# A Strassen feed-forward after sparse attention: the scheme used inside three chunks instead of four, with weight sums made one chunk later and fetched earlier

## The chip, the cores and the metric

One core of a Trainium2 chip runs one program that computes everything below. The metric is the device time of one execution in microseconds. Smaller is better.

## The reference, cut to what matters

```python
q, k, v: (8, 8, 576, 64)          # batch, heads, tokens, head width
mask_local   = (rel >= 0) & (rel < 32)                  # heads 0 to 3
mask_strided = (rel >= 0) & (pos_k % 32 == pos_q % 32)  # heads 4 to 7
attn = softmax(where(mask, q @ k.T / 8, -1e9)); y = attn @ v
x  = y.transpose(0, 2, 1, 3).reshape(8, 576, 512)
xn = (x - mean) / sqrt(var + 1e-6) * g_ln
out = x + relu(xn @ w_ch1) @ w_ch2        # 512 -> 2048 -> 512
```

## The kernel before, in words

The 4608 tokens are nine chunks of 512: chunks 0 to 7 are the first 512 tokens of each batch, chunk 8 gathers the last 64 of all eight. The layer norm is folded into the first weights and into a factor on each output row, so that a chunk needs only x, transposed, as TensorE's moving operand. For float32 accuracy each operand is split into a high and a low part, and every product is three matmuls: high by high, high by low, low by high. The 2048 hidden units are 16 blocks f. A plain step (`plain`, one f) runs 12 matmuls of 512 columns into `ph` (the first layer), has ScalarE write `hh` (relu, high part) and VectorE `hl` (low part), and runs 12 matmuls of 512 columns for the second layer of the block before (`run_groups`, tiles `po`). `ph` has one buffer.

Chunk 0 and chunk 1 are plain in the kernel before. Chunks 2 to 5 compute their first layer by Strassen's scheme alone, inside the chunk (`pair`): two blocks f together, tokens in two halves of 256 columns, seven products of six 256-column matmuls each (`product2`, tiles `x`) instead of eight, with sums of weight blocks as some stationary operands. Chunk 6 is plain; chunks 7 and 8 use the scheme on both chunks together.

The sums of weights (`w_sums`) are made by GpSimd in chunk 1, eight times six instructions, from tiles of the pool `tkp` (seven buffers), and stored to DRAM (`sd`); `a_store` stores the low parts of other weight blocks (`ad`) to make room, and `move`, on ScalarE, copies a weight half once that store has landed. Later, `stage_w(n)` fetches a set of sums from `sd` into a `tkp` tile `sw`, and `split_w(n)` splits it: ScalarE writes the high part, GpSimd the low part.

Attention of the batch that the chunk after next needs runs in between: four pieces a chunk, each for a pair of heads (`now` for its products with v, `nxt` for its scores). A piece is, in order: scores and products on TensorE into `m` and `n` (`s_blocks`, `v_blocks`); on VectorE the masks (`s_mask`), the maximum, and the division by the sums (`v_divide`, tile `xo`); GpSimd subtracts, ScalarE takes the exponential; VectorE transposes the result by 32-blocks and SyncE (SP) stores it (`p_turned`, DRAM tensor `pd`); `p_load` reads it back as `pt`, which the next piece's products need; `v_store` stores `xo` to DRAM (`xdl`, `xds`), and `x_raw` reads that back transposed for `x_blocks`. In plain chunks a generator (`pieces`) hands out these steps, four to each f; a short piece takes three f, a long one four.

The order of instructions on each engine is that of the code. The DMAs of SP's queue, and those that ScalarE issues, are issued in that order too, and an issuing engine stands still until what the next DMA waits for has come.

Within one `pair(c, p)` the order is: for even p the piece; products a11 (into tile x1), s2 (x2), s1 (x3), then a12 onto x1, s3 onto x2, a22 (x4, in x1's bank) and s4 onto x3, with one group of second-layer matmuls after each and two at the end. `Quarter` writes a quarter of the hidden block from x1 (`q`), from sums in SBUF (`q22`, `q21`) or from `u2` (`late`): the high part on ScalarE, `low()` on VectorE. VectorE's sums `add2` build `u2`, `u3` and `p1`.

Of the kernel before, what the change touches and what calls it, by code (L numbers as in the profile page):

```python
# [9 lines left out]
F32 = mybir.dt.float32  # L10
# [53 lines left out]
def kernel(  # L64
# [268 lines left out]
    class Pair:  # L333
# [84 lines left out]
        def t_piece(self):  # L418

            if self.local:  # L420
                self.qt, self.kt = qt_l, kt_l
                nc.vector.transpose(qt_l[:, 0:S], self.raw[:, 0])
                nc.vector.transpose(kt_l[:, STR:STR + S], self.raw[:, 1])
            else:
                self.qt, self.kt = qt_s, kt_s
                for i, dst in enumerate((qt_s, kt_s)):
                    nc.vector.transpose(
                        dst[:, 0:S].rearrange("p (r t) -> p t r", t=NB),
                        self.raw[:, i].rearrange("p (t r) -> p t r", r=STR))

# [160 lines left out]
        def x_raw(self, eng):  # L591

            self.xraw = tkp.tile([P, CH], F32, tag="tk", name=f"xraw{self.id}")
            x_b = (xd_l if self.local else xd_s)[self.b]
            for j in range(4):
# [6 lines left out]

        def x_blocks(self, xT=None):

            cc = self.h0 // 2
            if xT is not None:
# [5 lines left out]
            else:  # L612
# [3 lines left out]
                if d == 0 and (self.b > 2 or j):  # L616
                    stage_sums(j)
# [455 lines left out]
    def pieces(i0, i1):  # L1073
        for i in range(i0, i1):
            now = pairs[i] if i >= 2 * NHP else None
            nxt = pairs[i + 1] if i + 1 < NP else None
            short = i < 3 * NHP - 1 or i >= NP - NHP
# [32 lines left out]
            elif now:  # L1110
                now.x_blocks()
            yield
            yield
            yield
            if not short:
# [3 lines left out]
    gen = pieces(2 * NHP - 1, 3 * NHP)  # L1119
# [53 lines left out]
    def s_split(n):  # L1173
# [5 lines left out]
    xa_t = [xtp.tile([P, NCC, CH], F32R, tag=t, name=f"{t}_a") for t in ("xh", "xl")]  # L1179
    low1 = [w1s[f][:, :, 0:HC] for f in range(1, NFC, 2)]  # L1180
    high1 = [w1s[f][:, :, HC:CH] for f in range(1, NFC, 2)]
    slots = dict(zip(("s2", "s1", "s3", "s4"), (*(t[:, 3].rearrange("p (i x) -> p i x", i=2) for t in xa_t),
                                               *low1[6:])))
# [30 lines left out]

    def half_c(c, step):

        if c == 1:
            at, late = (10, 11, 12, 13), 2
        elif c < wide - 1:
            at, late = (4, 5, 8, 9), 2  # L1220
        else:
            at, late = (4, 5, 7, 8), 3
        if step in at:
            res[c].append([x_load(c, at.index(step))])
        if step - late in at:
            i = at.index(step - late)
            res[c][i].append(x_scale(res[c][i][0], f"{c}_{i}"))
# [20 lines left out]
    def plain(c, n_end):  # L1248
        for f in range(NFC):
            if c == 1 and f == NFC - 1:  # L1250
# [330 lines left out]
```

## Time and profile before

| | us |
|---|---|
| median of the runs | 970.07 (969.98 to 970.16, 2 runs) |
| the profiled execution | 968.79 |
| its span, first to last instruction | 967.0 |
| TensorE busy in the span | 889.5 (92%) |
| VectorE, ScalarE, GpSimd busy | 550.8, 285.5, 353.6 |
| mean granted clock of TensorE | 0.975 of full speed |

Busy times are sums over the whole span; what stands still where is seen only by cutting the span into the chunks' stretches.

### The profile page before, as it was taken

The page shows a single profiled execution, that of the slowest core. Times are in us where ns is not written, and L with a number is a line of the kernel's source. Part 1 is how long each engine was busy: PE and PEld are TensorE (multiplying, and loading weights), DVE is VectorE, ACT ScalarE, POOL GpSimd, SP SyncE. Part 2 cuts the span into 40 slices and gives each one's busy share as a digit, 9 for nine tenths or more (in the row PEclk, how much of TensorE's full clock was granted, in tenths as well). Part 3 has the DMA queues.
Part 4 walks back from the last instruction along what each step waited for, and adds up shares of the span by engine and source line. Part 5 has one row for each costly group of instructions (what it writes and reads, how often), then busy time and mean ns, then how long its engine had stood idle before and what let it go on. Part 6 is the DMA issues. An engine that isn't in the chain of part 4 may idle for free. (4 is left out here: it accounts for less than half of the span.)

```text
span 967.0 us, 20717 instructions
## 1 busy us (share of the span) xinstructions
PE 889.5 (92%) x7981; PEld 739.1 (76%) x7981; DVE 550.8 (57%) x1167; ACT 285.5 (30%) x590; POOL 353.6 (37%) x424
## 2 busy tenths in 40 slices
PE   7899998998799988999899988998979999999997
PEld 6688886786587777887677777777868887878786
DVE  6799954544565657556566557456645544242443
ACT  4786621111232233222422233222212221211121
POOL 5787745565434345243524244232202011112000
PEclk9899999999799999999999999999989999999999
DMA  9999664888677567866677666867676425331021
GB/s 185 230 275 275 178 109 113 203 178 201 125 202 160 142 138 180 203 141 146 138 206 153 150 132 194 187 137 185 164 170 121 96 87 160 102 102 63 1 87 44
DMA packets 383850, 146.64 MB, mean 152 GB/s; under 512 B 297860, under 2 KB 362248, under 8 KB 383752
## 3 DMA queue, kind: packets, MB, share of 16 engines
q1 hardware_dynamic: 300424, 130.44, 53.7%
q10 hardware_dynamic: 83328, 14.89, 8.5%
q8 instruction: 63, 1.03, 0.4%
q14 instruction: 35, 0.29, 0.1%
HBM read 104.56 MB, written 40.70 MB: 150 GB/s over the span
## 5 line engine op out<-in xcount | busy, mean ns | idle before, releaser
L903 PE MATMUL po<-w,hq 128*128 128x512 f32 x768 | 215.1, 396 | 10.7 <-ACT hq L1314 5.6
L903 PE MATMUL po<-w,hh 128*128 128x512 f32 x640 | 204.1, 401 | 0.0
L903 PEld LDWEIGHTS po<-w,hq 128*128 128x128 f32 x768 | 130.1, 190 | 28.5 <-ACT hq L1314 7.5
L903 PEld LDWEIGHTS po<-w,hh 128*128 128x128 f32 x640 | 121.3, 193 | 25.3 <-issue 0.3
L1301 PE MATMUL x<-xh_b,w 128*128 128x256 f32 x512 | 114.3, 286 | 18.0 <-DVE hq L1317 16.5
L903 PE MATMUL po<-w,hl 128*128 128x512 f32 x320 | 126.9, 396 | 0.0
L1301 PEld LDWEIGHTS x<-xh_b,w 128*128 128x128 f32 x512 | 88.1, 190 | 30.7 <-DVE hq L1317 22.0
L1245 POOL TENSOR_TENSOR w<-sw,w 128x256 fp32r<-128x256 f32 x64 | 46.4, 746 | 110.0 <-ACT w L1244 105.9
L498 POOL TENSOR_TENSOR sm<-sm,mx 128x640 f32<-128x640 f32 (+1 forms) x31 | 39.3, 1269 | 100.9 <-DVE mx L493 61.8
L871 DVE SCALAR_TENSOR_TENSOR hl<-ph,hh 128x512 fp32r<-128x512 f32 x48 | 32.9, 686 | 71.6 <-ACT hh L866 71.6
L1301 PE MATMUL x<-xl_b,w 128*128 128x256 f32 x256 | 72.2, 282 | 0.0
L903 PEld LDWEIGHTS po<-w,hl 128*128 128x128 f32 x320 | 61.4, 192 | 13.4
L1245 POOL TENSOR_TENSOR xh_a<-sw,xh_a 128x256 fp32r<-128x256 f32 x32 | 23.6, 737 | 129.2 <-ACT xh_a L1244 118.0
L744 POOL TENSOR_TENSOR rs<-rs,mhalf 128x1 f32<-128x1 f32 x36 | 20.2, 560 | 128.2 <-DVE rs L743 128.1
L866 ACT ACTIVATE hh<-ph 128x512 fp32r<-128x512 f32 x48 | 28.5, 594 | 106.4 <-PE ph L861 87.6
L1301 PEld LDWEIGHTS x<-xl_b,w 128*128 128x128 f32 x256 | 48.7, 190 | 4.7
L854 PE MATMUL ph<-xh,w 128*128 128x512 f32 x124 | 49.8, 401 | 0.0
L504 ACT ACTIVATE sm<-sm 128x648 f32<-128x648 f32 (+1 forms) x32 | 23.8, 744 | 87.3 <-POOL sm L498 87.3
L1176 POOL TENSOR_TENSOR rings<-stage,rings 128x512 fp32r<-128x512 f32 x16 | 20.6, 1289 | 77.8 <-ACT rings L1175 77.8
L854 PE MATMUL ph<-xl,w 128*128 128x512 f32 x124 | 48.4, 391 | 0.0
L1317 DVE SCALAR_TENSOR_TENSOR hq<-p,hq 128x256 fp32r<-128x256 f32 x32 | 16.0, 500 | 54.0 <-ACT hq L1314 54.0
L1244 ACT ACTIVATE xh_a<-sw 128x256 fp32r<-128x256 f32 x32 | 13.4, 417 | 96.0 <-DMA sw<-sd 90.9
(228 smaller groups left out, 1858.4 us busy)
## 6 DMA issues: line engine op xcount, KB each, us to landing
s<-in_moe_w_ch_dram SPq DMA_DIRECT2D x32, 512.0 KB
sw<-sd SPq DMA_DIRECT2D x64, 256.0 KB
out_dram<-x SPq DMA_DIRECT2D x32, 256.0 KB
raw<-in_q_dram SPq DMA_DIRECT2D x108, 72.0 KB
raw<-in_k_dram SPq DMA_DIRECT2D x108, 72.0 KB
wd<-w SPq DMA_DIRECT2D x24, 256.0 KB
ringa<-wd SPq DMA_DIRECT2D x24, 256.0 KB
xds<-xo SPq DMA_DIRECT2D x32, 162.0 KB
```

The source lines that it names most:

```text
L498: eng.tensor_tensor(out=sm, in0=sm, in1=mx[:, :, 0:nt].unsqueeze(3).broadcast_to([P, 2, nt, sm.shape[3]]), op=ALU.subtract)
L504: nc.scalar.activation(out=self.smv, in_=self.smv, func=AF.Exp, scale=SCALE)
L744: nc.gpsimd.tensor_tensor(out=rs, in0=rs, in1=mhalf, op=ALU.pow)
L854: nc.tensor.matmul(ph, w1h[:, cc], x[:, cc, :], start=(new and n == 0 and i == 0), stop=False)
L866: nc.scalar.activation(out=hh, in_=ph, func=AF.Relu)
L871: nc.vector.scalar_tensor_tensor(out=hl, in0=ph, scalar=0.0, in1=hh.bitcast(F32), op0=ALU.max, op1=ALU.subtract)
L903: nc.tensor.matmul(po[c, i], hx, w, start=(n_po[c, i] == 0 and n == 0), stop=(n_po[c, i] == NFC - 1 and n == 2))
L1176: nc.gpsimd.tensor_tensor(out=t[:, :, 1], in0=stage[n], in1=t[:, :, 0].bitcast(F32), op=ALU.subtract)
L1244: nc.scalar.activation(out=w[:, 0], in_=t[:, k], func=AF.Copy)
L1245: nc.gpsimd.tensor_tensor(out=w[:, 1], in0=t[:, k], in1=w[:, 0].bitcast(F32), op=ALU.subtract)
L1301: nc.tensor.matmul(ps, wx, xx[:, j], start=(start and j == 0 and i == 0), stop=(j == 1 and i == 2), skip_group_check=not start)
L1317: nc.vector.scalar_tensor_tensor(out=self.h[1], in0=self.src, scalar=0.0, in1=self.h[0].bitcast(F32), op0=ALU.max, op1=ALU.subtract)
```

## The change

Chunk 2 becomes a plain chunk, and Strassen's scheme alone starts with chunk 3 (`FIRST`). The sums of weights are made in chunk 2 instead of chunk 1, at f = 1, 2, 5, 6, 7, 9, 10, 11 instead of 0, 1, 3, 4, 6, 7, 9, 10; the moves of weight halves stay at f = 3, 7 and 11. In the pairs, `stage_w` for a set of sums is issued one pair earlier; `x_raw` is issued in two halves and lands in `xo` for batches 4 to 6; the divisions that read bank `n` come ahead of the masks; the two transposes of q and k stand on both sides of `q.low()`; `v_sums` stands behind `q22.low()`; the row statistics of two token blocks stand together. The whole weights are stored three times a chunk instead of twice. In chunk 6 the first and the last piece are long instead of short.

```diff
-            for j in range(4):
+            for j in js:
...
+        def x_room(self):
+            if 3 < self.b < B - 1:
+                self.xraw = self.xo.rearrange("p t h d -> p (t h d)")[:, 0:CH]
+            else:
+                self.xraw = tkp.tile([P, CH], F32, tag="tk", name=f"xraw{self.id}")
...
-            short = i < 3 * NHP - 1 or i >= NP - NHP
+            short = i < 3 * NHP - 1 or i in (29, 30)
+            later = i in (3 * NHP, 3 * NHP + 1)
...
-    gen = pieces(2 * NHP - 1, 3 * NHP)
+    gen = pieces(2 * NHP - 1, 4 * NHP)
...
+    LOADS.update({2: (12, 13, 13, 14), **{u: (4, 5, 8, 9) for u in range(FIRST, wide - 1)}})
+    SCALES.update({2: (14, 15, 15, NFC), **{u: (7, 7, 11, 11) for u in range(FIRST, wide - 1)}})
...
-            if c == 1:
+            if c == 2:
                 if f in SUMS_AT:
...
-    SUMS_AT = 0, 1, 3, 4, 6, 7, 9, 10
+    SUMS_AT = 1, 2, 5, 6, 7, 9, 10, 11
+    plain(1, NT)
...
-    plain(1, 1)
+    plain(2, 1)
...
+            now.v_divide(av[0:2])
+            if not nxt.local:
+                parts[0:2] = parts[1], parts[0]
             nxt.s_mask(parts)
-            late_low()
-            now.v_divide(av)
+            now.v_divide(av[2:])
             now.v_store()
             nxt.s_max()
-        else:
-            late_low()
+        late_low()
...
+        if n + 3 < n_end:
+            stage_w(n + 3)
         run_groups(1)
...
-        if fetch:
-            stage_w(n + 2)
...
-        if not even:
-            pairs[i + 2].t_piece()
+        turn = pairs[i + 2].t_pieces() if not even else iter(())
+        next(turn, None)
         run_groups(1)
         product2(p, "a12", "b21", x1, False)
         q = Quarter(c, 2 * p, 0, x1)
         q.low()
-        if fetch:
-            split_w(n + 2)
+        next(turn, None)
         if even:
             nxt.p_turned()
+        if n + 2 < n_end:
+            split_w(n + 2)
+        if even:
+            now.x_raw(nc.scalar, range(2))
...
+        q22 = Quarter(c, 2 * p + 1, 2, p1_t)
         if even:
-            now.x_raw(nc.scalar)
-        q22 = Quarter(c, 2 * p + 1, 2, p1_t)
+            now.x_raw(nc.scalar, range(2, 4))
...
-        if fetch:
-            stage_w(n + 3)
...
-        if even:
-            nxt.v_sums()
         add2(u3_t, x4, u3_t)
         q21 = Quarter(c, 2 * p + 1, 0, u3_t)
         q22.low()
+        if n + 4 < n_end:
+            stage_w(n + 4)
+        if even:
+            nxt.v_sums()
...
-    for c in range(2, wide - 1):
+    for c in range(FIRST, wide - 1):
```

Three places show how instructions moved.

The first is SP's queue in chunk 1, f = 0 to 2: `sd` and `ad` are the stores of the sums and of weight halves, `out_dram` the results of chunk 0, `pd` and `pt` the turned softmax of the next pair. Before:

```order
L814 DMA sd<-f_0_2199 128x2x256
L816 DMA sd<-f_0_2201 128x256 x2
L1230 DMA ad<-w_1_856 256x1x256
L880 DMA out_dram<-x_0_1846 128x512
L880 DMA out_dram<-x_1_1825 128x512
L880 DMA out_dram<-x_2_1793 128x512
L880 DMA out_dram<-x_3_1946 128x512
L628 DMA pd_206<-sm_192 32x4x192 x4
L642 DMA pt_2_2256<-pd_206 128x6x32 x4
```

The same queue now, in chunk 1 and then in chunk 2, f = 1 and 2:

```order
L893 DMA out_dram<-x_3_1946 128x512
L641 DMA pd_206<-sm_192 32x4x192 x4
L655 DMA pt_2_2242<-pd_206 128x6x32 x4
...
L641 DMA pd_207<-sm_191 32x4x160 x4
L363 DMA raw_1_3309<-in_q_dram 32x18x32 x4
L363 DMA raw_1_3309<-in_k_dram 32x18x32 x4
L827 DMA sd<-f_0_3318 128x2x256
L829 DMA sd<-f_0_3320 128x256 x2
L1243 DMA ad<-w_1_856 256x1x256
L827 DMA sd<-f_1_3363 128x2x256
L829 DMA sd<-f_1_3365 128x256 x2
L1243 DMA ad<-w_3_1033 256x1x256
```

No store of sums is left in chunk 1; in chunk 2 the first ones stand behind the `pd` stores of their step, and a piece has four steps instead of three until its `pt` is read.

The second place is ScalarE in an even pair (chunk 4, p = 2); `w` and `xh_a`, `xl_a` are the high parts that `split_w` writes, `hq` the quarters, `xraw` or `xo` the target of `x_raw`. Before:

```order
L1348 COPY p_2144<-x_4_2_6299 128x256
L1244 ACTIVATE w_13_1844<-sw_6188 128x256
L1244 ACTIVATE w_15_2016<-sw_6188 128x256
L504 ACTIVATE sm_191<-sm_191 128x2x6x54
L1314 ACTIVATE hq_4_0_6352<-x_4_2_6299 128x256
L1244 ACTIVATE xh_a<-sw_6331 128x256
L1244 ACTIVATE xl_a<-sw_6331 128x256
L600 DMA xraw_0_6375<-xdl 32x16x32 x4
L1314 ACTIVATE hq_5_2_6380<-p_2144 128x256
```

Now:

```order
L1369 COPY p_2142<-x_4_2_5940 128x256
L1257 ACTIVATE w_13_1844<-sw_5763 128x256
L1257 ACTIVATE w_15_2016<-sw_5763 128x256
L507 ACTIVATE sm_191<-sm_191 128x2x6x54
L1334 ACTIVATE hq_4_0_5993<-x_4_2_5940 128x256
L1257 ACTIVATE xh_a<-sw_5843 128x256
L1257 ACTIVATE xl_a<-sw_5843 128x256
L604 DMA xo<-xdl 32x16x32 x2
L1334 ACTIVATE hq_5_2_6018<-p_2142 128x256
L604 DMA xo<-xdl 32x16x32 x2
```

Two of the four DMAs now stand behind `hq_5_2` (`q22`); the tiles `sw` are the same in kind, but their DMAs stand half a pair to a pair earlier on SP.

The third place is VectorE in an odd pair (chunk 4, p = 3): `staged` is `x_blocks`, `qt_l` and `kt_l` the transposes of `t_piece`, `hq_6_0` is `q.low()`, BN the row statistics. Before:

```order
L615 STREAM_TRANSPOSE staged_2685<-xraw_0_6375 128x256 x2
L739 BN_STATS st_0_6459<-x_0_6328 128x6
L741 BN_AGGR mv_0_6461<-st_0_6459 128x2
L743 TENSOR_SCALAR rs_0_6463<-mv_0_6461 128x1
L422 STREAM_TRANSPOSE qt_l<-raw_1_6179 128x576
L423 STREAM_TRANSPOSE kt_l<-raw_1_6179 128x576
L1317 SCALAR_TENSOR_TENSOR hq_6_0_6489<-x_4_3_6424,hq_6_0_6489 128x256
```

Now:

```order
L628 STREAM_TRANSPOSE staged_3656<-xo 128x256 x2
L427 STREAM_TRANSPOSE qt_l<-raw_1_5820 128x576
L1337 SCALAR_TENSOR_TENSOR hq_6_0_6121<-x_4_3_6064,hq_6_0_6121 128x256
L427 STREAM_TRANSPOSE kt_l<-raw_1_5820 128x576
```

One transpose and the statistics have left the place ahead of `hq_6_0`; both blocks' statistics now stand between `q22.low()` and the `add2` that reads x3.

## Rows read from the trace of the kernel before

**Rows 1.** Windows by stage: length, TensorE busy (instructions), granted clock, DMA share, GB/s.

```profile
143.61:251.26 107.65, 98.33 (x885) 0.95 0.71 170
251.26:367.47 116.21, 100.42 (x994) 0.94 0.68 152
367.47:473.81 106.34, 95.87 (x993) 1.00 0.70 164
473.81:582.72 108.91, 97.86 (x993) 0.98 0.69 160
582.72:692.79 110.07, 100.52 (x1013) 1.00 0.73 172
692.79:786.65 93.86, 88.71 (x770) 0.96 0.53 122
```

**Rows 2.** Windows of single plain steps: PE, PEld, DVE, ACT, POOL busy, clock, DMA.

```profile
174.84:180.29 5.45, 5.45 (x26) 4.50 (x24) 1.19 (x2) 1.74 (x3) 5.14 (x7) 1.00 0.57 153
734.53:741.96 7.43, 7.43 (x141) 6.03 (x140) 4.68 (x13) 1.27 (x3) 0.42 (x1) 1.00 0.45 93
708.61:723.65 15.04, 9.89 (x141) 7.81 (x140) 5.39 (x13) 1.86 (x3) 1.28 (x1) 0.77 0.73 171
```

**Rows 3.** Windows of an even and an odd Strassen pair of chunk 3.

```profile
395.77:407.01 11.24, 10.89 (x70) 9.54 (x67) 6.83 (x19) 2.13 (x5) 2.66 (x3) 1.00 0.96 238
407.01:421.74 14.73, 13.23 (x183) 10.97 (x182) 8.69 (x22) 5.17 (x14) 8.42 (x12) 1.00 0.74 151
```

**Rows 4.** Timeline of TensorE: first matmuls of two products of 256 columns.

```profile
402.10 0.28 PE L1301 MATMUL x<-xh_b,w 128*128 128x256 f32 x1
...
403.50 0.28 PE L1301 MATMUL x<-xh_b,w 128*128 128x256 f32 x1
```

**Rows 5.** Waits of TensorE in 143.61:251.26 (chunk 1): us, times, longest.

```profile
PE n L521 <- DMA pt<-pd: 9.3, 5, 3.8
```

**Rows 6.** Timeline in chunk 1: VectorE's turned softmax, SP's stores behind it.

```profile
154.33 0.97 DVE L624 STREAM_TRANSPOSE sm<-sm 128x768 f32<-128x768 f32 x1
...
156.72 0.39 SPq L814 DMA_DIRECT2D sd<-f  x1
...
161.15 2.43 SPq L628 DMA_DIRECT2D pd<-sm  x4
```

**Rows 7.** Window of GpSimd in chunk 1: one set of sums.

```profile
174.20:180.00 5.80, 5.49 (x8) 1.00 0.51 139
```

**Rows 8.** Timeline of ScalarE: the first move of a weight half.

```profile
177.33 0.63 ACT L1200 ACTIVATE w<-w 128x512 fp32r<-128x512 f32 x1 [12.82 <-DMA ad<-w]
```

**Rows 9.** Waits of TensorE in 251.26:367.47 (chunk 2): the first pieces' `pt`.

```profile
PE n L521 <- DMA pt<-pd: 2.6, 1, 2.6
PE n L521 <- DMA raw<-in_q_dram: 1.1, 1, 1.1
```

**Rows 10.** Waits of TensorE in 367.47:473.81 (chunk 3).

```profile
PE x L1301 <- DVE hq L1317: 3.8, 3, 1.8
PE m L452 <- DVE u L1306: 1.7, 2, 0.9
PE x L1301 <- DVE xo L571: 1.7, 3, 1.0
PE po L903 <- DVE x L877: 1.5, 1, 1.5
PE po L903 <- ACT hq L1314: 1.2, 2, 0.7
PE x L1301 <- DVE p L1306: 0.9, 1, 0.9
```

**Rows 11.** Timeline in chunk 3, p = 2 and 3: a fetch of sums, ScalarE behind it.

```profile
402.52 0.41 SPq L1238 DMA_DIRECT2D sw<-sd  x1
...
407.23 0.42 ACT L1244 ACTIVATE xh_a<-sw 128x256 fp32r<-128x256 f32 x1 [5.25 <-DMA sw<-sd]
...
409.56 0.42 ACT L1314 ACTIVATE hq<-p 128x256 fp32r<-128x256 f32 x1 [1.60 <-issue]
```

**Rows 12.** Timeline of VectorE in chunk 3, p = 3: a transpose ahead of `q.low()`.

```profile
414.21 0.77 DVE L422 STREAM_TRANSPOSE qt_l<-raw 128x576 f32<-128x576 f32 x1
```

More of the change, by code (lines that the diff above doesn't have):

```diff
@@ L418, in t_piece, with t_pieces @@
         def t_piece(self):
[L420 to L423, printed above, removed]
-            else:
-                self.qt, self.kt = qt_s, kt_s
-                for i, dst in enumerate((qt_s, kt_s)):
+            for _ in self.t_pieces():
+                pass
+        def t_pieces(self):
+            self.qt, self.kt = (qt_l, kt_l) if self.local else (qt_s, kt_s)
+            for i, dst in enumerate((self.qt, self.kt)):
+                if self.local:
+                    nc.vector.transpose(dst[:, STR * i:STR * i + S], self.raw[:, i])
+                else:
                     nc.vector.transpose(
@@ L589, in v_store, with x_raw @@
                     nc.sync.dma_start(x_b[c, :, :, cs], xov[64 * c:64 * c + GS, 0:nt])
-        def x_raw(self, eng):
-            self.xraw = tkp.tile([P, CH], F32, tag="tk", name=f"xraw{self.id}")
+        def x_raw(self, eng, js=range(4)):
+            if 0 in js:
+                self.x_room()
             x_b = (xd_l if self.local else xd_s)[self.b]
-            for j in range(4):
+            for j in js:
                 c0 = P * self.n0 + 32 * j
@@ L1109, in pieces @@
                 now.x_blocks(whole[f"b{1 + cc // 2}1{cc % 2}"])
-            elif now:
+            elif now and not later:
                 now.x_blocks()
@@ L1114, in pieces @@
             yield
+            if later:
+                now.x_blocks()
             if not short:
@@ L1213, in back @@
         nc.sync.dma_start(w1s[f].bitcast(F32)[:, :, HC:CH], wd[p][:, 2])
+    LOADS, SCALES = ({u: at for u in range(1, wide)} for at in ((4, 5, 7, 8), (7, 8, 10, 11)))
+    LOADS.update({2: (12, 13, 13, 14), **{u: (4, 5, 8, 9) for u in range(FIRST, wide - 1)}})
+    SCALES.update({2: (14, 15, 15, NFC), **{u: (7, 7, 11, 11) for u in range(FIRST, wide - 1)}})
     def half_c(c, step):
-        if c == 1:
[L1218 to L1227, printed above, removed]
+        for d, steps in ((c, step), (c - 1, step + NFC)):
+            for i in range(NT):
+                if LOADS.get(d, ())[i:i + 1] == (steps,):
+                    res[d].append([x_load(d, i)])
+                if SCALES.get(d, ())[i:i + 1] == (steps,):
+                    res[d][i].append(x_scale(res[d][i][0], f"{d}_{i}"))
     def a_store(p):
@@ L1249, in plain @@
         for f in range(NFC):
-            if c == 1 and f == NFC - 1:
+            if c == 2 and f == NFC - 1:
                 for name in OPERANDS[0:3]:
@@ L1255, in plain @@
             h = hh, h_low(c, f, ph, hh)
-            if c == 1 and f in MOVED:
+            if c == 2 and f in MOVED:
                 move(f)
@@ L1330, in pair @@
         last, more = p == NFC // 2 - 1, c < wide - 2
-        n = NFC * (c - 2) + 2 * p
-        fetch = n < NFC * (wide - 3) - 2
+        n = NFC * (c - FIRST) + 2 * p
+        n_end = NFC * (wide - 1 - FIRST)
         i = NHP * (c + 1) + p // 2
@@ L1387, in pair @@
         add2(p1_t, x3, u3_t)
+        q22 = Quarter(c, 2 * p + 1, 2, p1_t)
         if even:
-            now.x_raw(nc.scalar)
-        q22 = Quarter(c, 2 * p + 1, 2, p1_t)
-        if not even and i + 3 < NP:
+            now.x_raw(nc.scalar, range(2, 4))
+        elif i + 3 < NP:
             pairs[i + 3].load_qk()
-        if fetch:
-            stage_w(n + 3)
         if last:
```

28 lines of the change are left out of this document (18 added, 10 removed).

## The prediction

> **What bounds the kernel now.** I cut the span into the chunks' stretches first [rows 1], since the busy share of the whole says only that TensorE is busy most of the time. In every stretch TensorE is the engine with the most work, and in every stretch of chunks 1 to 5 it stands still or runs slowly for a good part. To see how much, I took undisturbed pieces of its work. A plain step without attention takes 5.45 us for 24 matmuls of 512 columns, 0.227 us each; with a piece of attention it takes 7.43, so a piece costs 1.98 [rows 2]. Two successive Strassen products begin 1.40 us apart [rows 4]; less three matmuls of 512 columns that leaves 0.72 for six of 256 columns, 0.120 each.
>
> From these I work out floors. A Strassen pair has 42 matmuls of 256 columns and 24 of 512: 5.04 + 5.45 = 10.49; eight pairs and four pieces make 83.9 + 7.9 = 91.8 for a chunk. A plain chunk is 16 x 5.45 + 7.9 = 95.1. Against 91.8 the Strassen chunks take 116.2, 106.3, 108.9 and 110.1 [rows 1]; the last holds 7 groups more (7 x 0.68 = 4.8). The excess is 24.4, 14.5, 17.1 and 13.5. So each chunk in which the scheme stands alone is slower than a plain chunk without waits would be. Chunk 1, plain, has a floor of 94.0 for its stretch (15 steps, four and a half pieces, and 3.4 of the last step) and takes 107.65: an excess of 13.6.
>
> Then I asked what ended the waits. In chunk 1 all is `pt`: 9.3 us in 5 waits [rows 5], and the granted clock of 0.95 [rows 1] says that some of the stretch ran at 1.2 GHz instead of 2.4 after them. The timeline shows why: VectorE began to turn the softmax at 154.33, but SP issued its `pd` store only at 161.15, since the stores of the sums stood ahead of it from 156.72 on [rows 6]. In chunk 3 the waits are many and small: six kinds sum to 10.8 of the 14.5 [rows 10]; what is left is the restart after each.
>
> **The change part by part.**
>
> *Chunk 2 plain.* It removes 8 x 42 matmuls of 256 columns (336 x 0.120 = 40.3) and adds 192 of 512 (43.6): 3.3 us more on the path. By rows alone the scheme was worth that and no more here. The Trainium skill, "TensorE: Matmul & The Clock Gate", section "Wait — 56ns, not 53.3ns?", says that matmuls follow each other at the columns over 2.4 GHz plus about 2.5 ns. That would be an estimated 0.109 and 0.216 us, and giving up the scheme would cost an estimated 4.7 us; the rows show 0.120 and 0.227, so the sum goes by 3.3.
>
> *Chunk 1 without sums.* Eight sets of sums, 5.5 us of GpSimd each [rows 7], and 32 DMAs on SP leave it. `pd` then stands behind the four result stores alone, which are issued while the transposes still run; 6.8 us of lateness [rows 6] are more than the longest wait of 3.8 [rows 5]. I take 1 us of excess instead of 13.6; bounds 0 to 4 (one wait of the longest kind).
>
> *Chunk 2 with the sums.* The same work meets a plain chunk again, but a piece now has four steps until its `pt` is read, one step or 5.45 us more than the pieces of chunk 1 had, and the longest wait there was 3.8 [rows 5]; the first `sd` stores stand behind `pd`. What is late next is ScalarE: the first move of a weight half stood until 177.33, 12.8 us, for the `ad` store [rows 8], and the first sums now start one step later (f = 1) while the move stays at f = 3. Behind the move are queued the next `hh`, and on VectorE the transposes of the delayed `x_blocks`, which write into the freed half, and `hl`; `ph` has one buffer, so the next first layer waits for both. I expect short waits there, at f = 4 and f = 8. Bounds: nothing, and the 13.6 of chunk 1 before. I take 5, nearer the lower end, because GpSimd needs 8 x 5.5 = 44 us of a stretch of 93.
>
> *The first Strassen chunk.* Chunk 2 before has 24.4 of excess, 9.9 more than chunk 3; it starts with `pt` and `raw` waits of 2.6 and 1.1 us [rows 9] and a granted clock of 0.94 over the stretch [rows 1]. Now sums end at f = 11 and fewer loads stand ahead of the last `pd`. Bounds 0 and 9.9; I take 2.5, one wait like that of rows 9, since the same queues meet there.
>
> *The order in the pairs.* An even and an odd pair of chunk 3 take 11.24 and 14.73 [rows 3], against 10.49, and 12.47 with a piece: the odd pair, with three engines' queues full, loses most. I go through rows 10. `x <- hq` (3.8): x4 shares a bank with x1 and so waits for `q.low()`, which stood behind both transposes (0.77 us each [rows 12]) and behind `x_blocks`, itself late by the late `x_raw`; one transpose and the statistics leave, `x_raw` comes earlier: 1.0 remains, at p = 7, where the splits of the next chunk stand. `x <- xo` (1.7): x2 needs bank `n`, which the divisions now free first: 0.3. `po <- hq` (1.2): ScalarE waited 5.25 us for `sw`, fetched 4.7 us before, then issued four DMAs, and `q22` came at 409.56 [rows 11]; fetched a pair (over 10 us) ahead it doesn't wait: 0. `m <- u` (1.7): the next piece waits for the last `add2`; two blocks' statistics now stand ahead of it at p = 3 and 5. One block's take about a microsecond by their place in the order, which no row isolates; bounded by one transpose below and two above, I add 0.6 twice and remove little: 2.7. `po <- x` (1.5) stays, `x <- p` (0.9) halves. Together 6.0, and a restart of 0.25 for each of six (3.7 over 12 waits before, part of it owed to waits too small for these rows): 7.5 a chunk instead of 14.5. Bounds 4 and 14.5.
>
> The earlier fetches cost SP no extra DMA. Their price, if any, is a buffer: with four `x` tiles and a staged sum held, two of the seven are left for `sw`, and SP stands still until GpSimd has released one. `pd` is queued behind them. The cover is the half pair (5 us) that GpSimd has; I cost it at nothing.
>
> *Chunk 6.* The long first piece gives `pt` one step more. The stalled step takes 15.04 instead of 7.43, at a clock of 0.77 [rows 2]: 7.6 to win. The tail loads now stand ahead of the next piece's `pd`, which may give some back: bounds 0 and 7.6, I take 6.
>
> **The sum**, in the profiled execution's time. Chunk 1 starts at 143.61 [rows 1]. Chunk 1 up to chunk 2's first step: 16 x 5.45 + 4.5 x 1.98 = 96.1; chunk 2 up to chunk 3's first piece: 15 x 5.45 + 7.9 + 3.4 = 93.1. With 1, 5 and 2.5 of excess chunk 3 starts at 341.3 (367.47 before). Three Strassen chunks at 91.8 + 7.5 are 297.9, the leftover groups 4.8: 644.0 (692.79 before). Chunk 6 is 93.9 - 6 = 87.9, and what follows stays at 967.0 - 786.65 = 180.35. The span is 912.2. The execution was 1.8 longer than its span, and the runs' median 1.3 above that execution: **915 us**.
>
> **The rivals.**
>
> *Chunk 2 inherits it all*: the sums' stores keep SP busy ahead of `pd`, the move holds ScalarE, and the first Strassen chunk starts as before: 13.6 + 9.9 in place of 7.5. For it: the same GpSimd work, the same queue, a move with less time. Against it: the longer pieces. 915 + 16 = 931.
>
> *The pairs' waits only change places*: the new order makes others late, or the fetch isn't ahead at all, because its buffer is released only by the split before it, so that the change doesn't do what it says. Excess 14.5 in each of three chunks: 915 + 21 = 936. The Trainium skill, "DMA: Bandwidth & Descriptors", section "Latency and other measured facts", puts a DMA's fixed cost near 2 us. By that a set of sums would be there well before the split asks, and fetching it earlier would win little; the trace disagrees, with 4.7 us from issue to use in rows 11.
>
> *It goes better*: 1 us of excess in chunk 2, 1 at the start of chunk 3, and 4 a chunk: 915 - 4 - 1.5 - 10.5 = 899.
>
> *Slower*: SP stands for a `tkp` buffer ahead of `pd` in most pieces, `pt` is late, and each piece costs what the stalled step in chunk 6 did, 7.6 [rows 2]. Sixteen pieces lie in chunks 2 to 5; 8 late ones bring 915 + 61 = 976. It decides when SP issues `pd` a whole pair (10.5 us) behind the transposes. Against it: `pd` stands ahead of the second fetch, and the first needs only a split that GpSimd has begun.
>
> **How the numbers follow.** The forecast of 915 (some 906 to 924) gets 0.50, the better case 0.17, the heavy chunk 2 0.17, the waits that stay 0.12 (with both of these, 952, inside them at 0.02), slower 0.04. The range holds the better case and the two worse ones about their middles: 896 to 937; some 0.07 lie below, 0.08 above. Two per cent, about what a measurement of this kernel can tell from no change, is 951 or 989: faster 0.94, within 0.04, slower 0.02.
>
> **What would show it.** Right: no wait for `pt` in chunk 1, which ends near 240; chunk 3's first piece near 341; stretches of 98 to 101 in the Strassen chunks; no `po <- ACT hq` wait; no `x <- xo` wait over 0.3; no wait of 5 us in chunk 6. Wrong: `pt` waits in chunk 2, an `m <- u` wait over 1 us at p = 3 and 5, or ScalarE standing in the split for `sw` as before. The forecast fails most easily by the size of chunk 2's excess, which no row of a plain chunk with longer pieces shows.

## The result, and the profile after

The changed kernel takes 919.3 us (917.6 to 921.0, 2 runs) where the kernel before took 970.07: a ratio of 0.948, with a 95% interval of 0.940 to 0.955. That is faster. The profiled execution took 921.0 us with a span of 919.2 and a mean granted clock of 0.986. The forecast was 915, with a range of 896 to 937.

The sum came out 4 us low, but its terms did not come out equally well, and the stretches show which. Part of the nearness is luck: the span is 7.0 us over the 912.2 of the sum, and the runs' median then lies 1.7 below the profiled execution, where the sum had added 1.3. These are windows by stage of the kernel after: length, the busy times of PE, PEld, DVE, ACT and POOL, then granted clock, DMA share and GB/s; the boundaries are the same events (chunk 1's first step, the first pieces of chunks 2 to 5, chunk 6's first step and its last).

```profile
142.04:240.84 98.80, 98.80 (x906) 80.92 (x904) 53.43 (x110) 15.84 (x25) 8.56 (x9) 1.00 0.64 131
240.84:335.46 94.62, 92.24 (x829) 75.39 (x828) 44.44 (x91) 15.29 (x26) 54.50 (x60) 0.98 0.75 180
335.46:439.74 104.28, 95.17 (x994) 83.16 (x993) 70.28 (x170) 33.73 (x87) 50.63 (x61) 0.98 0.79 186
439.74:536.38 96.64, 93.11 (x992) 82.07 (x992) 66.10 (x160) 31.71 (x83) 43.35 (x52) 1.00 0.80 187
536.38:637.32 100.94, 98.34 (x1014) 85.79 (x1014) 67.63 (x158) 30.73 (x81) 35.60 (x42) 1.00 0.80 180
637.32:738.69 101.37, 92.33 (x769) 73.36 (x768) 49.04 (x103) 18.77 (x33) 12.32 (x12) 0.95 0.49 113
```

Chunk 1's stretch is all work: 98.80 us long and TensorE busy for 98.80. No wait for `pt` is left of the 9.3 us of [rows 5]. (It ends 2.8 us behind chunk 2's first step; in the kernel before, where chunk 2 began with a pair, it ended within chunk 1's last step. So the floor is 98.9 here and was 94.0 there.) Chunk 2 became 21.6 us shorter, chunk 4 became 12.3 shorter. Chunk 3 became only 2.1 shorter, and chunk 6, which was 93.86 [rows 1], became 7.5 us longer.

What is left to wait for is seen in TensorE's waits (total us, times, longest). In chunk 2, in chunk 4 and in chunk 6 of the kernel after:

```profile
PE ph L867 <- DVE hl L884: 2.4, 1, 2.4
...
PE m L455 <- DVE u L1326: 2.2, 3, 0.9
PE x L1321 <- DVE p L1326: 0.8, 1, 0.8
PE x L1321 <- DVE hq L1337: 0.7, 1, 0.7
...
PE ph L867 <- DVE hl L884: 5.9, 5, 2.5
PE n L524 <- DMA pt<-pd: 3.2, 2, 3.0
```

Of the six kinds of wait in [rows 10] three remain in chunk 4. `x <- xo` and both waits of `po` are gone, `x <- hq` is at p = 7 alone.

Windows of single steps and pairs of the kernel after, in this order: chunk 2's step f = 5, the first pair of chunk 3, an even and an odd pair later in that chunk (the last two answer to [rows 3]).

```profile
271.86:279.07 7.21, 7.21 (x24) 5.76 (x25) 4.40 (x12) 1.35 (x2) 4.92 (x5) 0.76 0.56 112
337.93:356.03 18.10, 12.77 (x67) 10.65 (x68) 10.82 (x29) 4.27 (x11) 11.48 (x13) 0.91 0.54 141
392.91:403.51 10.60, 10.60 (x72) 9.54 (x67) 8.27 (x22) 3.70 (x10) 4.28 (x5) 1.00 0.57 132
403.51:416.43 12.92, 12.44 (x184) 10.91 (x182) 8.30 (x19) 3.41 (x10) 3.97 (x6) 1.00 0.78 210
```

An even pair now runs without any wait at 10.60 us; an odd one takes 12.92 with half a microsecond of waiting, 1.8 less than before. The first pair of chunk 3 takes 18.1, which is 7.5 more than the other even pairs. SP's and VectorE's timelines there show what held it:

```profile
335.41 0.50 SPq L745 DMA_DIRECT2D x<-xdl  x1
...
340.44 0.69 DVE L752 BATCH_NORM_STATS2 st<-x 128x6 f32<-128x512 f32 x1 [2.56 <-DMA x<-xds]
...
342.24 0.69 DVE L752 BATCH_NORM_STATS2 st<-x 128x6 f32<-128x512 f32 x1 [0.71 <-DMA x<-xds]
...
343.88 0.61 DVE L574 TENSOR_TENSOR xo<-n,den 128x320 f32<-128x320 f32 x2
```

The division at 343.88 frees the bank that the second product needs. It stood behind two blocks' statistics, and these behind rows that SP began to load only at 335.41. TensorE waited 5.02 us for `xo`, and the pair's mean granted clock is 0.91:

```profile
PE x L1321 <- DVE xo L574: 5.0, 1, 5.0
```

In chunk 2, ScalarE's move of a weight half stood for its `ad` store, and the wait for `hl` at f = 5 came behind it:

```profile
269.80 0.63 ACT L1214 ACTIVATE w<-w 128x512 fp32r<-128x512 f32 x1 [9.80 <-DMA ad<-w]
```

In chunk 6, VectorE stood still at the turn of the first of the last rows (`turn(2)`, L1148), and the low half of the step stood behind it; SP had issued the eight loads for it late, over 6 us:

```profile
667.19 0.71 DVE L1148 STREAM_TRANSPOSE whole_b<-xt 128x512 f32<-128x512 f32 x1 [6.78 <-DMA xt<-xds]
667.82 0.65 DVE L884 SCALAR_TENSOR_TENSOR hl<-ph,hh 128x512 fp32r<-128x512 f32 x1
```

```profile
659.27 6.02 SPq L773 DMA_DIRECT2D xt<-xds  x8
```

In the kernel before the same turn stood at the end of the stalled step and waited 1.31 us: the attention product's wait for `pt`, which the change took away there, had covered it.

```profile
722.86 0.71 DVE L1132 STREAM_TRANSPOSE whole_b<-xt 128x512 f32<-128x512 f32 x1 [1.31 <-DMA xt<-xds]
```

But the turn's long wait by itself held TensorE for only 0.4 us. The longer of the waits came later: 2.5 us at 682.23, for a low half that stood behind the split `half_b` of the turned rows, which ScalarE ran only after standing for the DMAs of `x_raw`; 1.1 at 698.50, behind the next such splits; and 3.0 for `pt` at 710.60. The first, 1.6 at 660.46, lies ahead of the turn.

```profile
668.53 0.50 PE L867 MATMUL ph<-xh_b,w_5b 128*128 128x512 f32 x1 [0.38 <-DVE hl L884]
...
680.22 0.63 ACT L720 ACTIVATE half_b<-whole_b 128x512 fp32r<-128x512 f32 x1 [7.07 <-DMA xraw<-xdl]
...
682.23 0.72 PE L867 MATMUL ph<-xh_b,w 128*128 128x512 f32 x1 [2.46 <-DVE hl L884]
```

### The profile page after: what moved, and what is told of

It reads as the page before. It is cut to its first block, busy times and chain, and to the rows that moved or that the text cites. A ratio compares the mean times of both kernels' runs of the same rounds, so it can differ in the third digit from the quotient of the medians.

```text
span 919.2 us, 20228 instructions
## 1 busy us (share of the span) xinstructions
PE 875.8 (95%) x7837; PEld 730.0 (79%) x7837; DVE 534.9 (58%) x1108; ACT 264.7 (29%) x531; POOL 323.7 (35%) x380
## 4 chain that ended last, share of the span: by engine, by line
PE 31%; DMA 9%; DVE 5%; SPq 3%; issue 1%; ACT 1%; ACTq 0%; POOL 0%; DVEq 0%; POOLq 0%
PE po L916 16%; PE x L1491 7%; PE x L1321 4%; DMA pd<-sm 2%; PE ph L867 1%; DMA v_l<-in_v_dram 1%; DMA pt<-pd 1%; SPq L773 1%; DMA x<-xds 1%; PE m L455 1%; DVE hz L1510 1%; DVE u L1326 1%; PE ph L874 1%; PE n L524 1%; DMA v_s<-in_v_dram 1%
## 5 line engine op out<-in xcount | busy, mean ns | idle before, releaser
L916 PE MATMUL po<-w,hh 128*128 128x512 f32 x768 | 241.2, 396 | 0.0
L916 PE MATMUL po<-w,hq 128*128 128x512 f32 x576 | 160.2, 394 | 0.9 <-DVE x L890 0.7
L916 PE MATMUL po<-w,hl 128*128 128x512 f32 x384 | 150.6, 392 | 0.0
L916 PEld LDWEIGHTS po<-w,hq 128*128 128x128 f32 x576 | 97.4, 189 | 12.5 <-ACT w L1257 0.8
L1321 PE MATMUL x<-xh_b,w 128*128 128x256 f32 x384 | 84.3, 282 | 2.7 <-DVE p L1326 1.6
L916 PEld LDWEIGHTS po<-w,hl 128*128 128x128 f32 x384 | 72.7, 189 | 15.6
L867 PE MATMUL ph<-xh,w 128*128 128x512 f32 x188 | 75.2, 400 | 2.4 <-DVE hl L884 2.4
L867 PE MATMUL ph<-xl,w 128*128 128x512 f32 x188 | 74.0, 394 | 0.0
L1321 PEld LDWEIGHTS x<-xh_b,w 128*128 128x128 f32 x384 | 65.4, 188 | 10.0 <-issue 3.0
L874 PE MATMUL ph<-xh,w 128*128 128x512 f32 x188 | 51.2, 395 | 0.0
L867 PEld LDWEIGHTS ph<-xh,w 128*128 128x128 f32 x188 | 35.5, 189 | 10.1 <-DVE hl L884 2.8
L874 PEld LDWEIGHTS ph<-xh,w 128*128 128x128 f32 x188 | 35.7, 191 | 7.6
L867 PEld LDWEIGHTS ph<-xl,w 128*128 128x128 f32 x188 | 35.6, 189 | 7.1
```

Of the source, the lines that this page charges most:

```text
L867: nc.tensor.matmul(ph, w1h[:, cc], x[:, cc, :], start=(new and n == 0 and i == 0), stop=False)
L874: nc.tensor.matmul(ph, w1l[:, cc], xt[c][0][:, cc, :], start=False, stop=(cc == NCC - 1))
L916: nc.tensor.matmul(po[c, i], hx, w, start=(n_po[c, i] == 0 and n == 0), stop=(n_po[c, i] == NFC - 1 and n == 2))
L1321: nc.tensor.matmul(ps, wx, xx[:, j], start=(start and j == 0 and i == 0), stop=(j == 1 and i == 2), skip_group_check=not start)
```

## The experiments

All were run beside the kernel before on the same chip. The ratio to it is what is compared, since its median varied from 966 to 968 us among the chips of these runs.

| run | what differs from the changed kernel | median us | ratio | 95% interval |
|---|---|---|---|---|
| a0_after_again | nothing | 917.9 | 0.9486 | 0.9460 to 0.9511 |
| e1_short_pieces | chunk 6's pieces all short | 910.6 | 0.9407 | 0.9377 to 0.9437 |
| e2_turns_later | chunk 6's turns one step later | 907.4 | 0.9377 | 0.9353 to 0.9402 |
| e3_old_order | old fetch and old order in the pairs | 952.9 | 0.9834 | 0.9804 to 0.9864 |
| e4_old_fetch | old fetch, new order | 955.6 | 0.9872 | 0.9845 to 0.9899 |
| e6_fetch_alone | new fetch, old order | 922.0 | 0.9524 | 0.9495 to 0.9553 |
| e5_division_back | only the division's old place | 924.4 | 0.9545 | 0.9514 to 0.9576 |
| e8_stats_later | chunk 2's statistics later | 916.7 | 0.9472 | 0.9447 to 0.9498 |
| e9_sums_earlier | first sums one step earlier | 915.4 | 0.9466 | 0.9442 to 0.9491 |
| e10_together | three edits | 901.5 | 0.9325 | 0.9299 to 0.9350 |
| e13_stats_together | e10 with one more statistic moved | 899.0 | 0.9300 | 0.9266 to 0.9335 |
| e14_stats_spread | e13 with spread statistics | 895.9 | 0.9264 | 0.9233 to 0.9295 |

> The changed kernel as it is, beside the others on the same chip, to set their ratios against: by its first measurement 0.948 times the kernel before, here 0.945 to 0.951. Both theories expect the same.

It came out as expected. A ratio that is lower by 0.001 is worth 0.97 us in what follows.

**Chunk 6: two runs.**

```diff
-            short = i < 3 * NHP - 1 or i in (29, 30)
+            short = i < 3 * NHP - 1 or i >= NP - NHP
```

> Only the lengths of chunk 6's pieces are undone (all four of 11 calls again). In the trace after the change chunk 6 takes 101.4 us, where it took 93.9 before and 86 to 88 were forecast. Theory A: the longer pieces took away the stall of the attention product (5.15 us) behind which VectorE's wait for the last rows' loads was hidden before; VectorE's turn now waits 6.8 us in the open with the low halves queued behind it. Then chunk 6 goes back to 93 to 95 us, the AV product's wait for the turned p comes back, and the whole takes 911 to 913 us. Theory B: chunk 6 is slower for another reason (the transfers left over from the Strassen chunks, the earlier or later start of the stage), and the pieces' length does nothing: 917 to 921 us.

Measured: 7.6 us less. Chunk 6 takes 92.56 us, and its one wait is the old one, back again:

```profile
PE n L524 <- DMA pt<-pd: 4.8, 1, 4.8
```

VectorE's turn stands behind that step's masks and waits little, as before the change:

```profile
665.48 0.71 DVE L1148 STREAM_TRANSPOSE whole_b<-xt 128x512 f32<-128x512 f32 x1 [1.42 <-DMA xt<-xds]
```

So the longer pieces alone cost these 7.6 us, as theory A says, and the wait that they remove is worth less than what they bring. That the turn's wait is all of it, this run doesn't show.

```diff
-        3: [whole_tile(1, ("b220", "b120")), turn(2)],
-        4: [tail(0)],
-        5: [half_x(4, "b220")],
-        6: [turn(0), whole_tile(2, ...), whole_tile(3, ...), sums_x(0, nc.gpsimd)],
-        7: [half_x(5, "t10"), half_x(6, "t20"), tail(3)],
...
+        4: [whole_tile(1, ("b220", "b120")), turn(2)],
+        5: [tail(0)],
+        6: [half_x(4, "b220")],
+        7: [turn(0), whole_tile(2, ...), whole_tile(3, ...), sums_x(0, nc.gpsimd)],
+        8: [half_x(5, "t10"), half_x(6, "t20"), tail(3)],
```

(and so on up to f = 11, where `half_x(9)`, `tail(1)` and `s_fetch(0)` come together; lambdas left out.)

> The longer pieces of chunk 6 stay; the turn of the first half of the last rows and what hangs on it (the fetch, the half splits, the sums) stand one step of f later. Theory A (VectorE stands at the turn for data that come 6 us later, and what is queued behind it holds TensorE): the first wait of 1.6 us and the later ones of 2.5 and 1.1 us go, chunk 6 takes 88 to 94 us and the whole 906 to 912 us. Theory B (SyncE's queue is the limit: the last rows' loads stand ahead of the stores and loads of the turned p, wherever VectorE's turn stands): the wait of 3.0 us for p stays or grows, chunk 6 stays at 98 to 102 us and the whole at 916 to 921 us.

Measured: 10.5 us less. Chunk 6 takes 88.3, where the prediction had put 87.9, with the longer pieces kept. Of the 13.1 us by which the stretch is shorter, 7.4 are waits that are gone and 5.7 are less busy time (86.67 instead of 92.33, at a granted clock of 1.00 instead of 0.95). One wait is left, shown below the stretch:

```profile
639.12:727.43 88.31, 86.67 (x769) 70.55 (x768) 49.12 (x103) 19.22 (x33) 12.28 (x12) 1.00 0.57 130
```

```profile
PE ph L867 <- DVE hl L884: 1.6, 1, 1.6
```

Theory A holds in its sum, not in its detail. The first wait of 1.6, which I had put down to the turn, stays: there the low half follows a split of the first piece's rows (`xl<-whole_b`), which the longer piece brings into this step. What went is everything behind it. The edit moves the half splits and the later loads on SP as well as the turn, so it does not tell VectorE's part from ScalarE's or SP's: in this run SP issued the `pd` stores at 675.39, ahead of the second tail loads at 681.48; in the changed kernel it was the other way round.

**The pairs: four runs.** These take the change inside the pairs apart: the fetch of the sums, and the order of everything else.

```diff
                 if f == 15:
-                    stage_w(2)
...
-        if n + 3 < n_end:
-            stage_w(n + 3)
...
         half_c(c, 2 * p)
+        if n + 2 < n_end:
+            stage_w(n + 2)
...
+        if n + 2 < n_end:
+            stage_w(n + 3)
...
-        if n + 4 < n_end:
-            stage_w(n + 4)
```

That is the run with the old fetch.

> Only the fetch of the sums is put back to where it stood (a sum is fetched in the pair before its use; the third fetch at the end of chunk 2 goes); the order of VectorE's and ScalarE's work stays new. Theory A (ScalarE's split waited for its transfer, 5.25 us in one pair before, and held the other work of ScalarE): the waits on hq and u come back, 3 to 5 us a pair in some pairs, and the whole is 928 to 940 us. Theory B (the order on VectorE was what counted, ScalarE's wait lies in its slack): 917 to 922 us.

Measured: 37 us more, beyond theory A's end. The new order is all there, and only 12 of the 50 us are left. The run with the old order as well undoes, besides this, the division's place, the two turns around `q.low()`, the halves of `x_raw`, the places of `p_turned` and `v_sums` and the pairing of the statistics.

> The new plan of chunks (Strassen's scheme from chunk 3 on, sums in chunk 2) with the old order inside a pair of blocks: sums fetched inside the pair before, the division behind the low half, the turned rows in one piece, old places of the row loads, of the sums of p and of the statistics. Theory A (the order took the pairs' waits away: the excess over the floor in a Strassen chunk is 14.5 us in the old order and 5 in the new): chunks 3 to 5 take 24 to 30 us more and the whole 941 to 948 us. Theory B (the plan alone freed the pairs, since SyncE's and VectorE's work of the sums is no longer beside them, and the order adds little): 919 to 928 us.

Measured: 34 us more, a little beyond theory A's end. Its interval and that of the old fetch alone overlap: with the old fetch, no gain of the new order can be seen. Then the other way round, new fetch and old order (the diff of the run before without the lines of the fetch):

> The other way round than the run with the old fetch: the sums are fetched a pair ahead, as in the change, and the whole order of VectorE's and ScalarE's work inside a pair is put back (division behind the low half, turned rows in one piece, row loads, sums of p and statistics in their old places). The changed kernel took 917.9 us beside the last runs. Theory A (the order is worth something of its own: 0.6 us in each of 12 even pairs by the wait on xo, and the waits on hq in the odd ones): 925 to 930 us. Theory B (the fetch gives all of it, as far as the run with the old fetch says, which lost 38 us with the new order in place): 917 to 920 us.

Measured: 922.0, or 3.7 us more than the changed kernel, between the two theories; the intervals overlap, so that the order as a whole can't be told from nothing here either. By the ratios, the plan of chunks with the rest brings 16 us of the 50, the fetch 30 on top, the order the last 4, if they are that. The windows of the eight pairs of chunk 4 (from its first product to the next chunk's) tell the same of plan and fetch, in the order old order, old fetch, new fetch with the old order, changed kernel:

```profile
451.19:561.29 110.10, 98.95 (x999) 84.06 (x993) 66.08 (x159) 32.05 (x83) 42.91 (x54) 0.97 0.70 165
```

```profile
454.00:561.37 107.37, 95.40 (x999) 81.75 (x992) 67.81 (x159) 32.34 (x83) 43.38 (x53) 1.00 0.71 169
```

```profile
444.11:542.17 98.06, 94.10 (x999) 81.69 (x993) 65.33 (x159) 32.39 (x83) 42.00 (x53) 1.00 0.79 185
```

```profile
441.64:538.26 96.62, 93.09 (x1000) 82.05 (x993) 66.11 (x159) 31.71 (x83) 43.33 (x53) 1.00 0.81 187
```

Why the fetch does so much is seen in ScalarE's waits between 345 and 630 us. With the old fetch and the new order:

```profile
ACT xh_a L1257 <- DMA sw<-sd: 61.9, 17, 6.1
```

The kernel before has nearly the same:

```profile
ACT xh_a L1244 <- DMA sw<-sd: 61.5, 21, 6.1
```

In the changed kernel what is put down to `sw` in that stretch is

```profile
ACT hq L1334 <- DMA sw<-sd: 3.2, 1, 3.2
```

which is the wait of a quarter that reads no sums, and with the new fetch and the old order there is nothing. (One split of the changed kernel, in the first pair of chunk 3 and so ahead of that stretch, did wait 3.5 us.) With the old fetch ScalarE stood still for `sw` ahead of `xh_a` 17 times, up to 6.1 us each, and every `hq` stood behind that: of the quarter whose low half VectorE must write, of those that the groups of the second layer read, and of the one whose sum frees the bank of the next piece. One such pair (p = 5 of chunk 3, 20.06 us long) on SP and on ScalarE, with the old fetch:

```profile
409.57 1.74 SPq L813 DMA_DIRECT2D wd<-w  x3
411.41 0.95 SPq L1251 DMA_DIRECT2D sw<-sd  x1
```

```profile
417.63 0.42 ACT L1257 ACTIVATE xh_a<-sw 128x256 fp32r<-128x256 f32 x1 [5.86 <-DMA sw<-sd]
```

The fetch is issued behind three stores of whole weights and used 6.2 us after its issue. With the sums fetched a pair ahead, the same split waits for nothing. The fetch's new place also changes what stands behind it on SP; what that alone is worth, no run tells apart.

The last of the four puts only the division back behind the mask and the low half.

```diff
-            now.v_divide(av[0:2])
-            if not nxt.local:
-                parts[0:2] = parts[1], parts[0]
             nxt.s_mask(parts)
-            now.v_divide(av[2:])
+            late_low()
+            now.v_divide(av)
             now.v_store()
             nxt.s_max()
-        late_low()
+        else:
+            late_low()
```

> Of the changed kernel only the division's place is put back: VectorE divides behind the mask and the low half of the pair before, as it did. Theory A (the wait of 0.35 us on xo in the even pairs, and their 11.24 us instead of 10.6, come from this place alone): 12 even pairs of 0.6 us, 924 to 926 us. Theory B (the low half that then comes earlier gives it back in the groups behind it): 917 to 919 us.

Measured: 5.7 us more, as theory A says, with the place where it says. An even pair of chunk 3 is back at its old length:

```profile
369.82:381.06 11.24, 10.89 (x70) 9.54 (x67) 7.58 (x21) 3.16 (x8) 4.11 (x5) 1.00 1.07 238
```

That this one step measured more than the whole order (3.7) is within the uncertainty of the two. But the pairs show that part of the rest costs something. In the run with the new fetch and the old order an odd pair without a wait takes 12.46 us, in the changed kernel 12.92:

```profile
403.83:416.29 12.46, 12.46 (x183) 10.82 (x181) 8.06 (x19) 3.24 (x9) 3.98 (x6) 1.00 0.81 221
```

**The start of chunk 3 and the move in chunk 2.**

```diff
-    SCALES.update({2: (14, 15, 15, NFC),
+    SCALES.update({2: (14, NFC, NFC, NFC),
```

> Of the four statistics of chunk 2's residual blocks the second and third are taken in the first pair of chunk 3, after its second product, instead of at the end of chunk 2. Theory A (the first pair takes 18.1 us instead of 10.6 because VectorE's division stands behind statistics that wait for late rows): the first pair takes 11 to 14 us and the whole 913 to 916 us. Theory B (the next wait is as late: ScalarE's split of the fetched sums waits 3.5 us for its transfer at the same time, and the statistics only move in front of the second sum): the first pair stays above 16 us and the whole at 917 to 921 us.

Measured: 1.4 us less, within the uncertainty. The first pair falls to 13.9 us, as theory A says, since the division now stands at 338.72 and the late rows are met only behind it:

```profile
338.72 0.60 DVE L574 TENSOR_TENSOR xo<-n,den 128x320 f32<-128x320 f32 x2
...
345.73 0.69 DVE L752 BATCH_NORM_STATS2 st<-x 128x6 f32<-128x512 f32 x1 [1.80 <-DMA x<-xds]
```

The 3.3 us that the pair still has over 10.6 are other waits, the longest of 2.0 for `hq`. But the last pair of that chunk took 16.8 us in this execution instead of 14.6, which neither theory had named. In the later runs with the same edit it took 14.5 to 14.8, so it does not come with the edit each time.

```diff
-    SUMS_AT = 1, 2, 5, 6, 7, 9, 10, 11
+    SUMS_AT = 0, 1, 5, 6, 7, 9, 10, 11
```

> The first two of the eight sums of weights are made at f = 0 and 1 of chunk 2 instead of 1 and 2. Theory A (the 2.4 us wait and the half clock at f = 4, 5 come from the move at f = 3, whose copy on ScalarE waits for the store of the second sums, with VectorE's turn behind it): the excess of 4.3 us in these two steps falls to 0 to 1 and the whole to 914 to 916 us. Theory B (SyncE's queue takes the stores of sums ahead of the attention's transfers, and the wait appears one or two steps earlier, on p or on the rows): the chunk stays at 93 to 95 us or grows, and the whole at 918 to 924 us.

Measured: 1.9 us less, again within the uncertainty, and the wait at f = 5 is still there with 1.7 us. The excess of f = 4 and 5 fell from 4.3 to 2.2 us, not to 0 to 1, so theory A falls as to its edit; its cause is tested in the next run. SP shows why:

```profile
261.04 3.09 SPq L363 DMA_DIRECT2D raw<-in_k_dram  x4
...
265.73 0.54 SPq L1243 DMA_DIRECT2D ad<-w  x1
```

The store for which the move waits is issued at 265.73, in the changed kernel at 265.10: GpSimd made the sums earlier, but the store keeps its place behind SP's other issues.

**Together.** The two turns of the last rows later, one statistic moved, and the store itself moved instead of the sums:

```diff
             if c == 2:
+                if f == 0:
+                    a_store(0)
+                    a_store(1)
                 if f in SUMS_AT:
                     p = SUMS_AT.index(f)
                     w_sums(p)
-                    a_store(p)
+                    if p > 1:
+                        a_store(p)
```

> Three edits of the changed kernel together: the turns of the last rows one step later in chunk 6 (alone 907.4 us against 917 on that chip); the third of chunk 2's four statistics taken in the first pair of chunk 3; the copies of the first two low halves stored at f = 0 of chunk 2, since SyncE issued the store for which the move's copy waits behind 12 us of other issues. Theory A (three separate waits, each with its own cause): chunk 6 88 us, the first pair 13 to 15 instead of 18, no excess at f = 4, 5 of chunk 2; the whole 899 to 904 us. Theory B (time that is freed early is given back later, as the first pair's gain was at the end of chunk 3): 905 to 909 us.

Measured: 901.5, 15.6 us less than the changed kernel, as theory A says. SP issues both stores at 250.31, ScalarE's move doesn't wait any more, and no wait of TensorE is left in chunk 2:

```profile
250.31 1.88 SPq L1242 DMA_DIRECT2D ad<-w  x2
```

```profile
259.54 0.63 ACT L1213 ACTIVATE w<-w 128x512 fp32r<-128x512 f32 x1
```

The first pair still took 16.1; two of the four statistics still stand ahead of its division. With three of them in the first pair:

> The three edits together that took 901.5 us, with the second of chunk 2's statistics in the first pair of chunk 3 too (three of four there). Theory A (VectorE's division of the first pair then stands behind no late row: 13.9 us was measured for it with this edit alone, 16.1 with two of four): 899 to 901 us. Theory B (what the first pair gains is given back in the last pair of chunk 3, 16.8 us with this edit alone): 901 to 904 us.

Measured: 899.0, at the lower end; the step is within the uncertainty, but the first pair is 13.9 us and the last 14.8 in the trace. Then the statistics of chunks 3 to 5 apart again:

```diff
-    ... (7, 7, 11, 11) for u in range(FIRST, wide - 1)
+    ... (6, 7, 10, 11) for u in range(FIRST, wide - 1)
```

> The best kernel so far (three edits, 899.0 us) with the statistics of chunks 3 to 5 back in four places (steps 6, 7, 10, 11) instead of two by two (7, 11). Theory A (the waits of 0.4 to 0.9 us on u in the odd pairs come from two statistics that stand together in front of the second sum): pairs 3 and 5 of each chunk fall from 12.9 to 13.2 us to 12.5, six pairs, 2.5 to 3 us in all; the whole 896 to 897 us, less than the measurement can tell, so the pairs are read from the trace. Theory B (the waits come from the turned row pieces that stand there too): these pairs stay at 12.9 us.

Measured: 895.9; by the ratios 3.5 us less than the run before, within the uncertainty. Five of the six pairs fell to 12.4 to 12.5, as theory A says; the sixth (p = 5 of chunk 3) kept its wait of 0.5. Pairs 3 and 5 of chunk 3:

```profile
372.26:384.64 12.38, 12.38 (x184) 10.91 (x182) 8.05 (x20) 3.86 (x11) 7.01 (x10) 1.00 0.83 172
...
395.29:408.26 12.97, 12.44 (x184) 10.90 (x182) 8.33 (x19) 3.40 (x10) 3.98 (x6) 1.00 0.73 200
```

This version beats both kernels: 0.926 times the kernel before, 22 us under the change. Its stretches of chunks 2, 3 and 6:

```profile
241.66:331.99 90.33, 90.33 (x828) 74.31 (x828) 44.29 (x91) 15.30 (x26) 54.47 (x60) 1.00 0.79 189
331.99:431.45 99.46, 93.86 (x994) 82.12 (x993) 70.84 (x170) 33.61 (x87) 50.64 (x61) 1.00 0.83 195
...
625.70:712.64 86.94, 85.57 (x763) 69.35 (x762) 47.69 (x100) 17.60 (x30) 12.31 (x12) 1.00 0.56 127
```

## Why the prediction was right, and where it was wrong

*The plan of chunks.* The terms for chunks 1 and 2 held. Chunk 1 had an excess of 0 where 1 was taken; it takes 96.0 us from its first step to chunk 2's. Chunk 2 has 4.3 of excess where 5 was taken, by the mechanism named (ScalarE's move, the turns, the low half, the one bank of `ph`), at f = 4 and 5 alone; the wait at f = 8 did not come. Chunk 3's first piece came at 335.46 instead of 341.3: 1.6 of that came from chunk 0, whose work the change doesn't touch and whose end varies by some 2.5 us among the traces of the runs, 1.8 from these two terms, and 2.5 because the excess put at the start of chunk 3 came only behind the piece.

*The start of chunk 3* was under-sized: 7.5 us in the first pair instead of 2.5, inside the bounds of 0 to 9.9, by another wait than the one taken. The term took the `pt` wait of rows 9; what came was VectorE's wait for the statistics' rows, with the division behind it. Rows 9 show two of that stretch's eight kinds of wait, and this one stood in the same trace of the kernel before, among the others: the first pair of its first Strassen chunk took 17.7 us (257.62 to 275.34), nearly the 18.1 of now.

```profile
260.41 0.69 DVE L739 BATCH_NORM_STATS2 st<-x 128x6 f32<-128x512 f32 x1 [5.00 <-DMA x<-xds]
```

```profile
PE x L1301 <- DVE xo L571: 4.2, 4, 3.1
```

So the wait was not new: the change carried it over to the new first chunk, and moved the loads of these rows one or two steps later than they had stood in chunk 1.

*The pairs* were better than taken, and for another reason. 301.9 us were measured for the three chunks against 302.7; without the first pair's 7.5 that is 4.7 of excess a chunk instead of 7.5. The prediction spread the gain over the order: it put `x <- hq` down to the transposes, the statistics and `x_blocks` ahead of `q.low()`, and gave the fetch only the 1.2 us of `po <- ACT hq`. The runs turn that round. With the new fetch and the old order `x <- hq` is gone but for the pairs at a chunk's end and 0.5 us once; with the old fetch and the new order it stays mostly at the chunks' ends (up to 3.1 us) and turns up as a wait on `u` at p = 3 and 5, 0.9 to 5.4 us. The row for it stood in the prediction, 5.25 us of ScalarE's standing still in [rows 11], but it was counted for one `hq` instead of for all that is queued behind. The rival that an earlier fetch wins little is answered: 6.2 us passed from issue to use, and undoing the fetch cost 37 us. The Trainium skill ("DMA: Bandwidth & Descriptors", "Latency and other measured facts") puts a DMA's fixed cost near 2 us, by which the prediction had an earlier fetch win little. The trace disagrees with that use of it: the 6.2 us hold the transfer and its queue too. The terms for `xo` (0.3 left of 1.7 was taken, and none is seen behind the first pair) and for the statistics (two blocks together ahead of `m <- u`) were right in kind; one block's statistics take 1.1 us of VectorE (the row at 340.44 and its two small instructions), as bounded, and the wait on `u` at p = 3 and 5 was 0.4 to 1.0.

*Chunk 6* is the step that failed. The term was -6, with bounds of 0 and -7.6, and it measured +7.5: 13.5 of error, half of which hid behind 6.7 that the terms before it had too much; this is where the sum was lucky. The prediction saw that the tail loads stand ahead of the next piece's `pd` and let them give back some of the gain, but never more than it. It took the stalled step's 7.6 us as pure loss. But the stall was also a cover: VectorE's turn waited behind it for the last rows, and with the longer piece the turn comes first and waits in the open, 6.8 us, with the piece's masks and division late behind it and then the half splits; the second tail loads stand ahead of the next `pd`, as the prediction said. TensorE paid little at the turn itself (0.4 us) and the rest later, at the splits, at `pt` and in the clock. The run with the short pieces gives 7.6 us back, and with the turns and what hangs on them a step later the forecast 88 us appear (88.3).

Of the rivals none came as a whole, though the pairs came near the better case (4.7 of excess a chunk against 4): no `pt` wait is left in chunks 2 to 5. Two of the prediction's signs of being right failed: an `x <- xo` wait over 0.3 us came (5.0 in the first pair of chunk 3), and two of the Strassen stretches lie outside 98 to 101 (104.3 in chunk 3, 96.6 in chunk 4).

What stays open: how much of the plan's 16 us is chunk 2 without the scheme and how much the later place of the sums, which no run separates; why the last pair of a chunk still waits about 2 us (`p`, `u`, `hq`), and how much of chunk 6's loss was SP's order, how much ScalarE's and how much VectorE's.

## What to carry to other kernels

A wait in an in-order queue costs what stands behind it: count every instruction queued behind the waiting one, not only the one that waits, and put a fetch so far ahead that the engine that uses it never stands still. When a stall is removed, look at what else waited behind it, since a second wait that it covered may now lie open, and move that consumer, with what hangs on it, by the same step. Read all the waits of a stretch, not only those that the explanation needs. To make a store land earlier, move its issue on the queue, not the work that produces something else.

## What the runs showed of the hardware

The granted clock did not follow from a wait's length alone. After a wait of 2.4 us the step f = 5 of chunk 2 ran at a mean granted clock of 0.76, part of it at 1.2 GHz; when the changed kernel was run again, it did so after 2.1 us. At the same place in the run with the division put back, the wait was 2.5 us and the step kept the full clock. The repeated run first, then the division put back:

```profile
273.04:280.25 7.21, 7.21 (x24) 5.79 (x25) 4.72 (x12) 1.34 (x2) 4.92 (x5) 0.76 0.57 114
```

```profile
271.30:276.89 5.59, 5.59 (x25) 4.56 (x26) 3.41 (x11) 1.24 (x2) 3.46 (x3) 1.00 0.32 87
```

So nearly the same wait cost 4.3 us in the one (the excess of steps f = 4 and 5 over 7.43 and 5.45) and 2.8 in the other.
